# A first unit in another order, two transfers for the constants, and two later loads on another queue

## The chip, the cores and the metric

The kernel runs on one core of one Trainium2 chip. What counts is the device time of one execution in microseconds (us). The same program was timed three times, and the median stands for it. A fourth execution was taken with the hardware profiler, and all rows below come from that one.

## The reference

Three layers follow each other. First comes attention over 4 batches of 8 heads with 576 positions and 64 columns a head; heads 0 to 3 see the last 32 positions, heads 4 to 7 every fourth of the last 128. Then a layer takes the largest of three products, and a second layer uses a quotient of polynomials.

```python
def _attn_ref(q, k, v):
    scores = scale * np.matmul(q, k.transpose(0, 1, 3, 2))
    mask_plain = (rel >= 0) & (rel < window)                                  # window = 32
    mask_dil = (rel >= 0) & (rel < window * dilation) & (rel % dilation == 0) # dilation = 4
    ...
    attn = attn / (np.sum(attn, axis=-1, keepdims=True) + 1e-09)
    return np.matmul(attn, v)

x = _attn_ref(q, k, v)                       # as 2304 rows of 512
h = np.maximum(np.maximum(x @ w1, x @ w2), x @ w3)   # 512 to 768
x = h @ w_out                                        # 768 to 512
h = x @ w_in                                         # 512 to 2048
P = a[0] + a[1] * h + a[2] * h**2 + a[3] * h**3
Q = 1.0 + np.abs(b[0]) * np.abs(h) + np.abs(b[1]) * h**2
out = (P / (Q + 1e-06)) @ w_out2                     # 2048 to 512
```

## The kernel before

The 2304 rows are cut into 12 **chunks** of 192 rows, and two chunks make a **unit** of 384. While the matrix products of a unit run, the attention of the next one is mixed in between them. The first unit has nothing before it, so its order is written out by hand: `START` is a string of steps, and the program walks through it and issues each step's instructions on the engines that the step needs. Every engine then works its own instructions strictly in that order, and waits only for data. Chunks 0 and 1 are the first unit; chunks 2 and 3, which the second unit needs, are also done in `START`. From the second unit on, the order comes from the table `UNIT` and the loop behind it.

The names of the steps, where `c` is a chunk, `p` the plain heads, `d` the dilated ones:

- `Sc:g` scores on TensorE (lines 283 and 295). `MXc`, `Dc`, `SMc` are the maximum, the subtraction and the sum on VectorE (lines 321, 337, 356), `Ec` the exponential on ScalarE (345, 349), `SBc` the division by the sum on VectorE (363) or, with `act`, on ScalarE (367). `Xc` transposes on TensorE (374), `XCc` copies the result back (385, or 383 on VectorE). `Vc` multiplies by the values (397, 405); `VHc` and `VLc` split the outcome into a high and a low part on ScalarE (417) and VectorE (421).
- `L`, `up`, `bits`, `hi`, `lo` bring in one of the 24 weight blocks of the first two products. They come as 64-bit words of 512 KB: `L` loads on SyncE's queue (475), `up` (ScalarE, 488), `bits` (VectorE, two instructions, 494 and 496), `hi` (ScalarE, 510) and `lo` (VectorE, 518) turn them into a high and a low 32-bit part.
- `P:i` is one of the 18 groups of 12 products of 384 columns in the first unit (lines 535 to 537); `H:i` does half of one, the 192 columns of chunk 0 alone, and then `P:i` does only the other half. `M`, `HH`, `HL` take the largest (554, 556) and split it (560, 565). `Y` is the product by the fourth weight, 18 products each, `YS` its copy (589).
- `W:n` puts 4n products of a zero tile, `warm`, in front of the next step's own (line 180). Their result is overwritten.
- `qp`, `qd`, `kp`, `kd`, `k`, `v`, `mk` are loads of queries, keys, values and constants. `kp0` and `kp1` are the two parts of batch 0's plain keys.

SyncE's queue has eight semaphores for its transfers, taken in turn: the transfer n+8 is issued when transfer n has landed. Queries of chunks 4 and 5 and keys of batch 2 go out on GpSimd's queue, from calls that stand behind `START`.

Of the kernel before, what the change touches and what calls it, by code (L numbers as in the profile page):

```python
# [7 lines left out]
F32 = mybir.dt.float32  # L8
# [4 lines left out]
BF16 = mybir.dt.bfloat16  # L13
# [20 lines left out]


START = """
qp0 kp0 mk L W:19 S0:p,mm qd0 kd0 up MX0:p bits L E0:p qd1 hi W:10 S0:d,mm SM0:p L up lo
SB0:p,act MX0:d W:1 S1:d,sc qp1 D0:d bits kp1 E0:d X0:p,0,mm up X0:p,1,mm SM0:d v0 XC0:p,0 MX1:d
XC0:p,1 SB0:d W:9 S1:p,mm E1:d bits v1 W:1 X0:d,0,tp MX1:p W:2 V0:p,pv XC0:d,0 SB1:d hi W:2 X0:d,1,sc L
VH0:p D1:p W:1 X1:d,1,pv XC0:d,1 X1:d,0,tp XC1:d,1 VL0:p W:1 V0:d,mm L E1:p lo XC1:d,0 SM1:p L up  # L40
W:1 V1:d,pv SB1:p VH0:d up L VL0:d W:2 X1:p,0,mm VH1:d X1:p,1,sc bits XC1:p,0 H:0 L XC1:p,1 VL1:d hi
bits V1:p,mm L hi H:1 lo VH1:p qp2 VL1:p up lo hi P:0 k1 bits up S2:p,sc M:0 bits hi lo hi H:2
qd2 MX2:p up bits qd3 E2:p P:1 L lo M:1 P:2 lo L up hi S2:d,sc bits up L SB2:p,act bits P:3 L lo
hi M:2 L lo HH:0 P:4 hi HL:0 L M:3 lo up MX2:d up v3 M:4 P:5 up bits E2:d bits L P:6 bits hi L
hi M:5 X2:p,1,sc M:6 lo P:7 L XC2:p,1 lo up HH:1 L bits up X2:p,0,sc hi HL:1 P:8 v2 M:7 hi bits
XC2:p,0 SB2:d,act lo S3:d,sc lo L M:8 P:9 hi MX3:d L HH:2 lo up HL:2 L up bits X2:d,1,tp M:9
P:10 hi bits L XC2:d,1 lo hi qp3 X2:d,0,tp up M:10 P:11 L bits up XC2:d,0 E3:d bits P:12 M:11
SM3:d HH:3 hi HL:3 hi V2:p,sc lo M:12 P:13 up lo VH2:p bits up VL2:p hi V2:d,sc M:13 SB3:d,act
bits P:14 lo hi lo VH2:d lo up X3:d,0,mm M:14 P:15 XC3:d,0 bits HH:4 up HL:4 hi bits X3:d,1,pv
M:15 P:16 up lo hi bits hi M:16 P:17 lo VL2:d lo S3:p,sc M:17 XC3:d,1,dve HH:5 HL:5 V3:d,mm  # L50
MX3:p E3:p Y:0 VH3:d SM3:p SB3:p VL3:d X3:p,1,tp YS:0 Y:1 XC3:p,1 X3:p,0,sc YS:1 Y:2 XC3:p,0,dve
V3:p,mm YS:2 Y:3 VH3:p VL3:p YS:3
"""

UNIT = """
# [26 lines left out]
def kernel(  # L82
# [15 lines left out]
    nc = tc.nc  # L98
    B, H, S, D = BATCH, HEADS, SEQ, DIM
# [29 lines left out]
    QA = 2  # L129
# [14 lines left out]
    const = ctx.enter_context(tc.tile_pool(name="const", bufs=1))  # L144
# [51 lines left out]
    def load_k(b, part=None):  # L196

        if b not in at_k:
            at_k[b] = (
                at.tile([128, S // 32, 2, 32], F32, tag="kTp", bufs=2, name=f"kTp{b}"),  # L200
                at.tile([128, 8, S // 4], F32, tag="kTd", bufs=2, name=f"kTd{b}"),
            )
        kTp, kTd = at_k[b]
        queue = nc.sync if b < 2 else nc.gpsimd
        for k, cut in ((0, slice(0, CH // 32)), (2, slice(CH // 32, S // 32))):
            if part in (None, k):
                queue.dma_start(out=kTp[:, cut].rearrange("p n a t -> p (n a t)"),
                                in_=kp_in[b][:, 64 * cut.start:64 * cut.stop])
        if part in (None, 1):
            queue.dma_start(out=kTd.rearrange("p n m -> p (n m)"), in_=kd_in[b])  # L210

    def load_q(c, g):
        if c >= NCH:
            return
        queue = nc.sync if c < 2 * QA else nc.gpsimd
        if g == "p":
            t = at.tile([128, 2 * BP, 2 * QP], F32, tag="qTp", bufs=QA, name=f"qTp{c}")
            queue.dma_start(out=t.rearrange("p n w -> p (n w)"), in_=qp_in[c])
        else:
            t = at.tile([128, 8, 2 * M], F32, tag="qTd", bufs=QA, name=f"qTd{c}")  # L220
            queue.dma_start(out=t.rearrange("p n w -> p (n w)"), in_=qd_in[c])
        at_raw[c, g] = t
# [399 lines left out]
    with ExitStack():  # L622
        nc.scalar.preload_act_table_set("natural_log_exp_and_others")
        warm = const.tile([128, 128], BF16, name="warm")
        nc.vector.memset(warm, 0.0)
        mk = const.tile([128, 512], F32, name="mk")
        ident = mk[:, 0:128]
        mk16 = mk[:, 128:384].bitcast(BF16)
        mkd16 = mk[:2 * M, 384:512].bitcast(BF16)
        ident16 = mk16[:, 0:128]  # L630
        mP16 = mk16[:, 128:128 + BP * WP].rearrange("p (i w) -> p i w", i=BP)
        mD16 = mkd16[:, 0:2 * WD].rearrange("p (i w) -> p i w", i=2)
        co = mk[:, 464:470]
# [242 lines left out]
def _laid_out(inputs):  # L876

    import numpy as np

    q, k, v = inputs["q"], inputs["k"], inputs["v"]  # L880
    B, H, S, D = q.shape
    NP, CH, QP, M = H // 2, CHUNK, 64, CHUNK // 4
    BP, NC, WP, WD = CH // QP, S // CH, QP + 32, M + 32
    out = {}
    mk = np.zeros((128, 128 + BP * WP + 2 * WD), np.float32)
    mk[:, 0:128] = np.eye(128, dtype=np.float32)
    for i in range(BP):
# [5 lines left out]
    mk16 = np.zeros((128, 1024), np.int16)
    mk16[:, 0:256] = mk[:, 0:128].copy().view(np.int16)
    mk16[:, 256:256 + 128 + BP * WP] = _bf16(np, mk[:, 0:128 + BP * WP])
    mk16[0:2 * M, 768:768 + 2 * WD] = _bf16(np, mk[0:2 * M, 128 + BP * WP:])
# [77 lines left out]
```

## Time and profile before

| | us |
|---|---|
| median of three runs | 797.05 (796.89 to 797.38) |
| profiled execution, its own time | 796.7 |
| span of the profiled execution | 794.9 |
| TensorE busy | 788.3 |
| VectorE busy | 597.8 |
| ScalarE busy | 466.8 |

The span is what the profile covers from its first to its last record; the execution's own time holds 1.8 us more. TensorE is busy in 99% of the span, but its fillers count as busy, too, and its products overlap, so this share doesn't tell how much of the time is needed work.

### The profile page before, as it was taken

How to read it: one execution, taken by the hardware profiler on the slowest of the kernel's cores; microseconds unless marked ns; L12 is line 12 of the kernel's file. 1: busy time of each engine (PE TensorE's matmuls, PEld its weight loads, DVE VectorE, ACT ScalarE, POOL GpSimd, SP SyncE). 2: the span in 40 equal slices, each digit the busy share in tenths (PEclk: the TensorE clock that was granted, in tenths of full speed). 3: DMA queues.
4: the chain of work that ended last, by engine and by line, in shares of the span. 5: the costliest groups of instructions: out<-in, count | busy, mean ns of one | idle time of the engine just before them, and what ended most of it. 6: DMA issues, size and time to landing. Idle time of an engine off the chain costs nothing.

```text
span 794.9 us, 12837 instructions
## 1 busy us (share of the span) xinstructions
PE 788.3 (99%) x4976; PEld 721.6 (91%) x4976; DVE 597.8 (75%) x1068; ACT 466.8 (59%) x907; POOL 59.1 (7%) x113
## 2 busy tenths in 40 slices
PE   9999999999999999999999999999999999999998
PEld 9999999999999999999978888888888889999996
DVE  5999275566476565548299998888988888998996
ACT  5897232333333333255398768666786677777775
POOL 0100111211211111000100001000010001000000
PEclk9999999999999999999999999999999999999999
DMA  9992346655465454164500011000110011001001
GB/s 342 404 407 80 106 147 215 215 180 190 162 200 186 160 186 164 37 241 158 178 14 1 1 53 54 1 1 0 40 54 0 1 40 53 1 1 40 1 0 40
DMA packets 28061, 86.55 MB, mean 109 GB/s; under 512 B 3648, under 2 KB 4928, under 8 KB 28000
## 3 DMA queue, kind: packets, MB, share of 16 engines
q1 hardware_dynamic: 19056, 52.70, 18.8%
q0 software_dynamic: 8944, 33.04, 11.7%
q8 instruction: 39, 0.64, 0.3%
q14 instruction: 22, 0.18, 0.1%
HBM read 67.90 MB, written 17.83 MB: 108 GB/s over the span
## 4 chain that ended last, share of the span: by engine, by line
PE 80%; issue 10%; DVE 4%; ACT 3%; DMA 1%; POOL 1%; POOLq 0%; ACTq 0%; DVEq 0%; SPq 0%
PE acc L819 8%; PE acc L820 8%; PE acc L821 8%; PE mm L535 8%; PE mm L537 8%; PE mm L536 8%; PE h L537 8%; PE h L535 8%; PE h L536 8%; PE sc L295 3%; PE tpp L374 2%; PE sc L180 1%; PE pv L397 1%; PE pv L405 1%; DVE cvt L496 1%
## 5 line engine op out<-in xcount | busy, mean ns | idle before, releaser
L535 PE MATMUL mm<-x1h,w1s 128*128 128x384 f32 (+1 forms) x444 | 150.1, 339 | 0.0
L537 PE MATMUL mm<-x1h,w1s 128*128 128x384 f32 (+1 forms) x444 | 147.2, 332 | 0.0
L536 PE MATMUL mm<-x1l,w1s 128*128 128x384 f32 (+1 forms) x444 | 147.1, 331 | 0.0
L535 PE MATMUL h<-x2h,w2s 128*128 128x512 f32 (+1 forms) x320 | 118.0, 369 | 0.0
L537 PE MATMUL h<-x2h,w2s 128*128 128x512 f32 (+1 forms) x320 | 118.0, 369 | 0.0
L536 PE MATMUL h<-x2l,w2s 128*128 128x512 f32 (+1 forms) x320 | 117.7, 368 | 0.0
L819 PE MATMUL acc<-w2s,gh 128*128 128x512 f32 x288 | 112.8, 392 | 0.5 <-ACT gh L800 0.5
L820 PE MATMUL acc<-w2s,gh 128*128 128x512 f32 x288 | 113.1, 393 | 0.0
L821 PE MATMUL acc<-w2s,gl 128*128 128x512 f32 x288 | 109.0, 389 | 0.0
L768 ACT ACTIVATE q<-h 128x512 f32<-128x512 f32 (+1 forms) x80 | 44.4, 555 | 89.7 <-PE h L537 86.6
L535 PEld LDWEIGHTS mm<-x1h,w1s 128*128 128x128 f32 x444 | 83.2, 188 | 0.6
L536 PEld LDWEIGHTS mm<-x1l,w1s 128*128 128x128 f32 x444 | 83.6, 188 | 0.0
L537 PEld LDWEIGHTS mm<-x1h,w1s 128*128 128x128 f32 x444 | 83.4, 188 | 0.0
L775 DVE SCALAR_TENSOR_TENSOR q<-q,cs,ab 128x512 f32<-128x512 f32 (+1 forms) x80 | 55.8, 697 | 36.3 <-ACT ab L769 35.8
L535 PEld LDWEIGHTS h<-x2h,w2s 128*128 128x128 f32 x320 | 60.1, 188 | 9.1
L536 PEld LDWEIGHTS h<-x2l,w2s 128*128 128x128 f32 x320 | 60.1, 188 | 8.8
L537 PEld LDWEIGHTS h<-x2h,w2s 128*128 128x128 f32 x320 | 60.0, 188 | 7.8
L821 PEld LDWEIGHTS acc<-w2s,gl 128*128 128x128 f32 x288 | 54.1, 188 | 11.9
L819 PEld LDWEIGHTS acc<-w2s,gh 128*128 128x128 f32 x288 | 54.0, 188 | 11.6 <-ACT gh L800 0.9
L556 DVE TENSOR_TENSOR m<-mm,m 128x384 f32<-128x384 f32 x72 | 39.9, 554 | 31.5 <-PE mm L537 30.4
L820 PEld LDWEIGHTS acc<-w2s,gh 128*128 128x128 f32 x288 | 54.1, 188 | 9.9
L770 ACT ACTIVATE p<-h,cs 128x512 f32<-128x512 f32 (+1 forms) x80 | 59.1, 739 | 0.0
(100 smaller groups left out, 1441.3 us busy)
## 6 DMA issues: line engine op xcount, KB each, us to landing
w1r<-in_w_dram SPq DMA_DIRECT2D x18, 512.0 KB, 9.6
raw<-in_w_in_dram SPq DMA_DIRECT2D x16, 512.0 KB, 3.4
w2d<-cvt POOLq DMA_DIRECT2D x32, 256.0 KB, 2.5
raw<-in_w_out_dram SPq DMA_DIRECT2D x16, 512.0 KB, 3.5
w2s<-w2d SPq DMA_DIRECT2D x32, 256.0 KB, 4.7
x2d<-xs POOLq DMA_DIRECT2D x24, 192.0 KB, 2.4
vd<-in_vd_dram POOLq DMA_DIRECT2D x8, 512.0 KB, 5.0
out_dram<-ob POOLq DMA_DIRECT2D x15, 256.0 KB, 2.7
```

Of the source, the lines that this page charges most:

```text
L295: nc.tensor.matmul(o, lhsT=lq, rhs=rk, start=not pem, stop=not pem or n % G == G - 1)
L374: nc.tensor.transpose(tp[:, i, :], sv[:, G * j + i, :], ident[:Q, :Q])
L535: nc.tensor.matmul(o, lhsT=lh, rhs=rh, start=(i == 0), stop=False)
L536: nc.tensor.matmul(o, lhsT=lh, rhs=rl, start=False, stop=False)
L537: pe_at[0] = nc.tensor.matmul(o, lhsT=ll, rhs=rh, start=False, stop=(i == n - 1))
L556: nc.vector.tensor_tensor(out=m1[u, f], in0=o, in1=m1[u, f], op=ALU.max)
L768: nc.scalar.activation(out=s["q"], in_=s["h"], func=AF.Square)
L770: nc.scalar.activation(out=s["p"], in_=s["h"], func=AF.Identity, scale=cs[:, 3:4], bias=cs[:, 2:3])
L775: nc.vector.scalar_tensor_tensor(out=s["q"], in0=s["q"], scalar=cs[:, 5:6], in1=s["ab"], op0=ALU.mult, op1=ALU.add)
L819: nc.tensor.matmul(o, lhsT=gh, rhs=w[:, 0:512], start=(c == 0), stop=False)
L820: nc.tensor.matmul(o, lhsT=gh, rhs=w[:, 512:1024], start=False, stop=False)
L821: nc.tensor.matmul(o, lhsT=gl, rhs=w[:, 0:512], start=False, stop=(c == F2 - 1))
```

## The change

The kernel after has four edits.

1. `START` holds the same steps in another order. It has 31 instead of 49 `W` units (124 instead of 196 fillers), and no `H`: each of the 18 product groups runs with 384 columns at once. `SB2:d` moves from ScalarE to VectorE, `SB3:p` from VectorE to ScalarE, and two copies of chunk 3's transposes from VectorE to ScalarE.
2. The constants come in two transfers: masks and the 16-bit identity first (`mk`, 208 words a row), the 32-bit identity, the dilated mask and the coefficients second (`mkB`, 214 words a row), where there was one of 512 words.
3. Queries of chunks 4 and 5 and keys of batch 2 are issued on SyncE's queue instead of GpSimd's.
4. The tile `cs` has 24 instead of 8 words a row, so that the tiles of the left-hand pools stand 64 bytes further on.

```diff
 START = """
-qp0 kp0 mk L W:19 S0:p,mm qd0 kd0 up MX0:p bits L E0:p qd1 hi W:10 S0:d,mm SM0:p L up lo
...
+mk qp0 mkB kp0 W:14 S0:p qd0 MX0:p kd0 kp1 E0:p W:7 S0:d,mm qp1 SM0:p SB0:p,act MX0:d D0:d W:1 S1:p
...
@@ load_k
-        queue = nc.sync if b < 2 else nc.gpsimd
+        queue = nc.sync if b < 3 else nc.gpsimd
@@ load_q
-        queue = nc.sync if c < 2 * QA else nc.gpsimd
+        queue = nc.sync if c < 3 * QA else nc.gpsimd
@@
+        CUT = (128 + BP * WP) // 2
+        CW = CUT + 128 + WD + 6
         mk = const.tile([128, 512], F32, name="mk")
-        ident = mk[:, 0:128]
-        mk16 = mk[:, 128:384].bitcast(BF16)
-        mkd16 = mk[:2 * M, 384:512].bitcast(BF16)
+        mk16 = mk[:, 0:CUT].bitcast(BF16)
...
+        ident = mk[:, CUT:CUT + 128]
...
-            "mk": lambda: nc.sync.dma_start(out=mk, in_=consts),
+            "mk": lambda: nc.sync.dma_start(out=mk[:, 0:CUT], in_=consts[:, 0:CUT]),
+            "mkB": lambda: nc.sync.dma_start(out=mk[:, CUT:CW], in_=consts[:, CUT:CW]),
...
-        cs = const.tile([128, 8], F32, name="cs")
+        cs = const.tile([128, 24], F32, name="cs")
```

The lines of the kernel after are one lower than those of before (475 becomes 474, and so on).

SyncE's queue at the start of the program, before; `w1r` is a weight block, `kTp` and `kTd`, `qTp` and `qTd` keys and queries, plain and dilated, `vp` and `vd` the values, and the second number of a shape counts words a row.

```order
L218 DMA qTp_141<-in_qp_dram 128x768
L207 DMA kTp_143<-in_kp_dram 128x384
L635 DMA mk<-in_consts_dram 128x512
L475 DMA w1r_0_147<-in_w_dram 128x512
L221 DMA qTd_241<-in_qd_dram 128x768
L210 DMA kTd_144<-in_kd_dram 128x1152
L475 DMA w1r_1_251<-in_w_dram 128x512
L221 DMA qTd_259<-in_qd_dram 128x768
L475 DMA w1r_2_319<-in_w_dram 128x512
L218 DMA qTp_352<-in_qp_dram 128x768
L207 DMA kTp_143<-in_kp_dram 128x768
L237 DMA vp_371<-in_vp_dram 128x768
```

The same queue at the same place in the kernel after.

```order
L635 DMA mk<-in_consts_dram 128x208
L217 DMA qTp_142<-in_qp_dram 128x768
L636 DMA mk<-in_consts_dram 128x214
L206 DMA kTp_145<-in_kp_dram 128x384
L220 DMA qTd_220<-in_qd_dram 128x768
L209 DMA kTd_146<-in_kd_dram 128x1152
L206 DMA kTp_145<-in_kp_dram 128x768
L217 DMA qTp_276<-in_qp_dram 128x768
L220 DMA qTd_307<-in_qd_dram 128x768
L474 DMA w1r_0_334<-in_w_dram 128x512
L474 DMA w1r_1_340<-in_w_dram 128x512
L474 DMA w1r_2_342<-in_w_dram 128x512
```

All keys and queries of chunks 0 and 1 now stand ahead of the first weight block, which was fourth and is tenth.

VectorE from its first maximum on, before; `mx`, `sm`, `sb` are the maximum, the sum and the scores, `cvt` is a weight block being converted.

```order
L321 TENSOR_REDUCE mx<-sc 128x3 x2
L324 TENSOR_SCALAR mx<-mx 128x6
L494 TENSOR_SCALAR cvt<-cvt 128x512
L496 SCALAR_TENSOR_TENSOR cvt<-w1r_0_147,cvt 128x512
L356 TENSOR_REDUCE sm<-sb 128x6
L518 TENSOR_TENSOR w1s_0_261<-cvt,w1s_0_261 128x512
L360 TENSOR_SCALAR sm<-sm 128x6
L361 RECIPROCAL sm<-sm 128x6
L321 TENSOR_REDUCE mx<-sc 96x4 x2
L337 TENSOR_TENSOR sb<-sc,mx 96x4x48 x2
```

VectorE from its first maximum on, after; `spare` holds the scores of chunk 1.

```order
L320 TENSOR_REDUCE mx<-sc 128x3 x2
L323 TENSOR_SCALAR mx<-mx 128x6
L355 TENSOR_REDUCE sm<-sb 128x6
L359 TENSOR_SCALAR sm<-sm 128x6
L360 RECIPROCAL sm<-sm 128x6
L320 TENSOR_REDUCE mx<-sc 96x4 x2
L336 TENSOR_TENSOR sb<-sc,mx 96x4x48 x2
L320 TENSOR_REDUCE mx<-sc 128x3 x2
L336 TENSOR_TENSOR spare<-sc,mx 128x288 x2
L355 TENSOR_REDUCE sm<-sb 96x8
```

The conversion of the first block stood behind the first maximum; now the softmax of both chunks goes ahead of it.

TensorE at the end of `START`, before; `hh` and `hl` are the two parts of the largest, `wo1s` the fourth weight, and the last row is the second unit's first product.

```order
L295 MATMUL sc<-kTp_680,qTp_1079 128x96 x6
L405 MATMUL pv<-pt,vd_864 64x3x16 x16
L535 MATMUL mm<-hh_831,wo1s_1141 128x384
...
L374 MATMUL tpp<-mk,sb 96x128 x3
...
L397 MATMUL pv<-pt,vp_862 64x64 x12
...
L535 MATMUL mm<-x1h_689,w1s_0_261 128x384
```

TensorE at the end of `START`, after.

```order
L536 MATMUL mm<-x1h_149,w1s_2_1068 128x384
L404 MATMUL pv<-pt,vd_1084 64x3x16 x16
L396 MATMUL pv<-pt,vp_1082 64x64 x12
L534 MATMUL mm<-hh_730,wo1s_1104 128x384
...
L534 MATMUL mm<-x1h_529,w1s_0_489 128x384
```

Scores, transposes and values of chunk 3's plain heads stood among the four `Y`; now all attention ends ahead of the first `Y`, and nothing but `Y` stands between it and the second unit. From there on TensorE's rows are the same in both kernels.

## Rows read from the trace of the kernel before

**Rows 1.** Who TensorE waited for, whole span: total us, times, longest us.

```profile
PE sc L180 <- DVE warm L625: 1.0, 1, 1.0
PE tpp L374 <- DVE sb L363: 0.8, 1, 0.8
PE acc L819 <- ACT gh L800: 0.5, 1, 0.5
PE tpp L374 <- ACT pt L385: 0.4, 1, 0.4
```

**Rows 2.** Stretches: length, busy us (instructions) of each engine, granted clock, DMA share, GB/s.

```profile
1.00:5.00 4.00, 4.00 (x38) 4.00 (x39) 0.00 (x0) 1.02 (x1) 0.00 (x0) 1.00 0.77 228
5.00:7.00 2.00, 2.00 (x39) 2.00 (x37) 0.40 (x3) 0.00 (x0) 0.00 (x0) 1.00 0.96 336
25.58:78.77 53.19, 52.77 (x442) 50.76 (x441) 50.19 (x104) 44.14 (x122) 3.47 (x7) 1.00 0.73 289
```

**Rows 3.** TensorE's timeline: start us, us, line, operation.

```profile
0.99 6.31 PE L180 MATMUL sc<-warm 128*128 128x128 bf16 x76 [0.99 <-DVE warm L625]
7.14 0.41 PE L283 MATMUL sc<-mk 128*128 128x288 bf16 x2
...
26.08 0.33 PE L535 MATMUL mm<-x1h,w1s 128*128 128x192 f32 x1
...
27.57 0.92 PE L397 MATMUL pv<-pt,vp 96*64 96x64 f32 x24
...
31.19 0.42 PE L283 MATMUL sc<-mk 128*128 128x288 bf16 x2
...
32.70 0.34 PE L535 MATMUL mm<-x1h,w1s 128*128 128x192 f32 x1
...
36.78 0.43 PE L283 MATMUL sc<-mk 96*96 96x320 bf16 x2
...
38.36 0.42 PE L535 MATMUL mm<-x1h,w1s 128*128 128x384 f32 x1
...
46.79 0.49 PE L374 MATMUL tpp<-mk,sb 128*96 128x128 f32 x3
...
94.67 0.33 PE L535 MATMUL mm<-x1h,w1s 128*128 128x384 f32 x1
```

**Rows 4.** Transfers issued near 1.2 to 3.1 us: KB each, us from issue to landing.

```profile
kTp<-in_kp_dram SPq DMA_DIRECT2D x1, 192.0 KB, 3.1
mk<-in_consts_dram SPq DMA_DIRECT2D x1, 256.0 KB, 4.4
kTd<-in_kd_dram SPq DMA_DIRECT2D x1, 576.0 KB, 7.6
```

**Rows 5.** SyncE's queue in order of time: start us, us of the issue.

```profile
1.66 0.42 SPq L635 DMA_DIRECT2D mk<-in_consts_dram x1
2.12 0.43 SPq L475 DMA_DIRECT2D w1r<-in_w_dram x1
...
3.07 0.43 SPq L210 DMA_DIRECT2D kTd<-in_kd_dram x1
...
19.55 0.33 SPq L218 DMA_DIRECT2D qTp<-in_qp_dram x1
```

**Rows 6.** VectorE's timeline at the prices of its steps.

```profile
24.44 0.76 DVE L363 TENSOR_TENSOR spare<-spare,sm 128x576 f32<-128x576 f32 x1
...
35.64 0.56 DVE L556 TENSOR_TENSOR m<-mm,m 128x384 f32<-128x384 f32 x1
36.11 0.68 DVE L518 TENSOR_TENSOR w1s<-cvt,w1s 128x512 fp32r<-128x512 f32 x1
36.71 0.42 DVE L494 TENSOR_SCALAR cvt<-cvt 128x512 int32<-128x512 int32 x1
...
37.77 0.17 DVE L360 TENSOR_SCALAR sm<-sm 128x6 f32<-128x6 f32 x1
...
42.20 0.88 DVE L321 TENSOR_REDUCE mx<-sc 96x4 f32<-96x320 f32 x2
```

More of the change, by code (lines that the diff above doesn't have):

```diff
@@ L36 @@
 START = """
-qp0 kp0 mk L W:19 S0:p,mm qd0 kd0 up MX0:p bits L E0:p qd1 hi W:10 S0:d,mm SM0:p L up lo
[L38 to L52, printed above, removed]
+mk qp0 mkB kp0 W:14 S0:p qd0 MX0:p kd0 kp1 E0:p W:7 S0:d,mm qp1 SM0:p SB0:p,act MX0:d D0:d W:1 S1:p
@@ new lines @@
+qd1 S1:d,pv E0:d X0:p,1,mm MX1:p X0:p,0,mm L up D1:p L L SM0:d E1:p MX1:d v0 SM1:p SB0:d SB1:p v1
+XC0:p,1 qp2 L W:8 X0:d,1,mm up X0:d,0 XC0:p,0 W:1 X1:p,1,sc V0:p,mm X1:p,0,sc qd2 bits L L E1:d
+XC0:d,0 XC0:d,1 V0:d,mm up XC1:p,0 XC1:p,1 L SB1:d hi bits k1 X1:d,1,pv bits VH0:p VH0:d L qp3
+V1:p,tp X1:d,0,pv S2:p L hi lo XC1:d,1 VL0:p XC1:d,0 qd3 lo VL0:d up V1:d,mm VH1:p bits hi VH1:d
+VL1:p hi VL1:d lo S2:d,pv L P:0 L up MX2:d bits up P:1 E2:d lo bits M:0 up MX2:p M:1 P:2 SB2:d hi
+P:3 L X2:d,0,mm E2:p hi X2:d,1 bits L L M:2 lo hi lo up lo bits up HH:0 L hi bits L S3:d up lo
@@ new lines @@
+XC2:d,1 S3:p,pv bits up M:3 hi XC2:d,0 bits L hi lo P:6 M:6 P:4 hi P:5 up SB2:p,act MX3:d lo bits L
+v2 lo up hi MX3:p P:7 M:4 E3:d bits P:9 M:5 up lo X2:p,0 up XC2:p,0 SM3:d bits M:7 M:9 hi hi
+SB3:d,act lo HL:0 P:10 bits P:8 L lo X2:p,1,sc M:10 hi M:8 up up lo P:12 E3:p up bits L L bits hi
+P:13 SM3:p L bits lo M:12 hi P:14 HH:1 XC2:p,1 L P:15 lo up hi up HL:1 SB3:p,act v3 M:13 bits P:16
+M:15 hi M:14 V2:d,sc X3:d,0,mm lo up X3:d,1,pv HH:2 bits lo up hi M:16 XC3:d,0 P:11 bits hi XC3:d,1
+X3:p,0 HH:4 bits V2:p,sc X3:p,1,mm P:17 lo L lo M:11 up bits up HL:2 XC3:p,0 hi XC3:p,1 bits M:17
@@ L53 @@
+HH:3 hi HH:5 lo VH2:p lo HL:4 hi HL:3 lo V3:d V3:p,tp HL:5 VH2:d VH3:d VH3:p VL2:d Y:0 YS:0 Y:1 Y:2
+Y:3 VL3:p VL2:p YS:1 YS:2 VL3:d YS:3
 """
@@ L625 @@
         nc.vector.memset(warm, 0.0)
+        CUT = (128 + BP * WP) // 2
+        CW = CUT + 128 + WD + 6
         mk = const.tile([128, 512], F32, name="mk")
-        ident = mk[:, 0:128]
-        mk16 = mk[:, 128:384].bitcast(BF16)
-        mkd16 = mk[:2 * M, 384:512].bitcast(BF16)
+        mk16 = mk[:, 0:CUT].bitcast(BF16)
         ident16 = mk16[:, 0:128]
         mP16 = mk16[:, 128:128 + BP * WP].rearrange("p (i w) -> p i w", i=BP)
-        mD16 = mkd16[:, 0:2 * WD].rearrange("p (i w) -> p i w", i=2)
-        co = mk[:, 464:470]
+        ident = mk[:, CUT:CUT + 128]
+        mD16 = mk[:2 * M, CUT + 128:CUT + 128 + WD].bitcast(BF16).rearrange("p (i w) -> p i w", i=2)
+        co = mk[:, CUT + 128 + WD:CW]
         loads = {
-            "mk": lambda: nc.sync.dma_start(out=mk, in_=consts),
+            "mk": lambda: nc.sync.dma_start(out=mk[:, 0:CUT], in_=consts[:, 0:CUT]),
+            "mkB": lambda: nc.sync.dma_start(out=mk[:, CUT:CW], in_=consts[:, CUT:CW]),
             "kp0": lambda: load_k(0, 0), "kd0": lambda: load_k(0, 1), "kp1": lambda: load_k(0, 2),
@@ L892, in _laid_out @@
         mk[:2 * M, 128 + BP * WP + WD * i:128 + BP * WP + WD * i + WD] = np.concatenate([band, band])
[L893 to L896, printed above, removed]
+    cut = 128 + BP * WP
+    mk16 = np.zeros((128, cut + 256 + 2 * WD + 12), np.int16)
+    mk16[:, 0:cut] = _bf16(np, mk[:, 0:cut])
+    mk16[:, cut:cut + 256] = mk[:, 0:128].copy().view(np.int16)
+    mk16[0:2 * M, cut + 256:cut + 256 + 2 * WD] = _bf16(np, mk[0:2 * M, cut:])
     consts = mk16.view(np.float32)
-    consts[:, 464:468] = inputs["moe2_a"]
-    consts[:, 468:470] = inputs["moe2_b"]
+    at = (cut + 256 + 2 * WD) // 2
+    consts[:, at:at + 4] = inputs["moe2_a"]
+    consts[:, at + 4:at + 6] = inputs["moe2_b"]
     out["consts"] = consts
```

## The prediction

> **What bounds the kernel now.** I read the list of TensorE's waits first, then the stretches, then TensorE's own timeline, and VectorE's last.
>
> In the whole span TensorE waits four times for 2.7 us [rows 1], and none of it lies in the middle of the span. So after the first unit nothing but TensorE's own work sets the time, and whatever the first unit saves or loses is kept to the end, as long as its rows stay the same there. They do.
>
> In the first unit the picture has three parts [rows 3]. From 0.99 to 7.14 TensorE runs 76 fillers and waits for the first keys and queries. From 7.14 to 26.08 it does the attention of chunks 0 and 1 with fillers between the steps: the softmax on VectorE and ScalarE and the loads set the pace, and TensorE has little to do. From 26.08, where the first half group `H:0` starts, to 94.67, where the second unit's first product starts, it works without a gap but for two waits of 0.8 and 0.4 us [rows 1]. In almost the same stretch, 25.58 to 78.77, VectorE is busy 50.2 of 53.2 us [rows 2]. Two engines are thus nearly full here, and a change is worth what it brings on the later of the two.
>
> **The change part by part.**
>
> *Start.* 38 fillers stand between 1 and 5 us, 39 between 5 and 7 [rows 2]: 9.5 and 19.5 in a us. The granted clock reads 1.00 in both, so this is the step from 1.2 to 2.4 GHz after a stretch of steady products. 56 fillers in place of 76 end at 5.0 + 18/19.5 = 5.9. The scores `S0:p` also need the first keys, now the fourth transfer, issued where the weight block stood at 2.12 [rows 5]. At best it lands after the keys' own 3.1 us [rows 4], at 5.2; at worst like the old constants, with about the same bytes ahead, at 1.66 + 4.4 = 6.1 [rows 4, 5]. I take 6.0, 1.1 us earlier than 7.14.
>
> *Loads of the attention.* Before, 2.36 MB were issued up to the dilated keys, which landed at 3.07 + 7.6 = 10.7 [rows 4, 5]. The transfer issued at 19.55 is the 22nd, which waited for the 14th, so 5.90 MB had landed at 19.5 [rows 5]. That is 2.49 us for one MB. After, the bytes up to the dilated keys are 1.79 MB, so they land at 9.2; up to the plain queries of chunk 1, 2.58 MB, 11.2; up to its dilated ones, 2.97 MB, 12.2; the first weight block at 13.5, the values between 17 and 21.
>
> *The chain to the first full group.* A plain scores step takes 32.70 - 31.19 = 1.5 us, a dilated one 38.36 - 36.78 = 1.6 [rows 3]. `S1:p` starts at 11.2 with its queries and ends at 12.8, `S1:d` ends at 14.4. VectorE has then done the softmax steps that it could, and from 14.6 on it has no gap to `VL1:d`, the last thing that `P:0` needs. Its steps there, by their prices [rows 6]: `MX1:d` 0.88 and a small one, 1.0; `SM1:p`, priced as a maximum over its 576 columns, 0.8; `SB0:d`, `SB1:p`, `SB1:d`, scaled by columns from 0.76 with two small ones of 0.17, 0.85 + 1.1 + 1.2; four `bits` of 37.77 - 36.71 = 1.06, 4.2; two `lo` of 0.60, 1.2; four `VL`, priced as the `M` of the same 384 columns, 35.64 to 36.11, 0.47 each, 1.9. Together 12.25, so `P:0` starts at 26.9. TensorE is there in time: its steps of both chunks and `S2` make 15.7 us (six scores 9.3, eight transposes of about 0.3, four value steps of about 1), the 17 `W` behind the first 3.8, and 6.0 + 19.5 = 25.5.
>
> *What is left from there.* Before, 94.67 - 26.08 = 68.6 [rows 3]. Off go the two waits, 1.2; `V1:p`, 0.9, and the two scores of chunk 2, 3.1, which now stand ahead of `P:0`; and the halves: 36 products of 192 columns take 36.78 - 32.70 = 4.08, 0.113 each, 48 of 384 columns take 46.79 - 38.36 = 8.43, 0.176 each [rows 3], so 72 of the one cost 8.16 where 36 of the other cost 6.32, 1.8 more. 61.6 us remain. Without a wait the second unit starts at 26.9 + 61.6 = 88.5, 6.2 earlier.
>
> *VectorE's deadline.* The four `Y` now stand last, 18 products of 0.176 each, 12.6 together. The sixth sixth of the first one needs `HL:5` and the last `lo`: at 88.5 - 12.6 + 2.6 = 78.5. From 26.9 VectorE has 20 `bits` (21.2), 22 `lo` (13.2), 12 `M` and 6 `HL` (8.5) and the softmax of chunks 2 and 3 (7.0, four maxima 3.3, `SB2:d` 1.2, two sums 1.3, three pairs of small ones 1.2): 49.9, done at 76.8 if it never waits. Before, it stood idle 3.0 us of a like stretch [rows 2], mostly in small waits for ScalarE, which is busy 44.1 of the 53.2. Bounds: no idle time, no wait; 3.0 us, done at 79.8 and TensorE waits 1.3. I take 2.2, nearer to the row, since the order is new but the pairs of `up`, `bits`, `hi`, `lo` are the same: 0.5 us of waiting. The middle is as tight: `P:15` can start near 61.7, and its `lo` is done near 61.1 plus the idle time up to there.
>
> *Costed at nothing.* The moved copies, `SB2:d` and `SB3:p`: they are in the sums above on VectorE; ScalarE gives up one scaling in eight parts and gets one in six and two copies, about as much, and its 53.2 - 44.1 = 9 us of idle time [rows 2] cover the rest. The queries and keys on SyncE's queue: 2.75 MB behind the last weight block. All loads of `START` are 22.1 MB, so that block lands near 10.7 + 19.8 x 2.49 = 60, the moved ones near 67; the second unit asks for them after 88, so 20 us cover it, and the next weights behind them are asked for later still. If that cover were gone, the second unit's first scores would wait up to 7 us. The weight blocks come later at first (13.5), but the `lo` of the last has some 15 us in hand. The split constants: one issue more, 0.4 us on the queue [rows 5], in the 6.0 above; VectorE's coefficients need the second part, which lands ahead of the keys. The 64 bytes: no row shows the same operation on a tile at another offset, shapes and counts stay; I take nothing, with a few tenths either way.
>
> **Sum.** Start of the second unit: 88.5 + 0.5 = 89.0 for 94.67, 5.7 less. Against the profiled execution: span 794.9 - 5.7 = 789.2, its own time 791.0. It lies 0.35 below the median, so the median comes out at 791.3.
>
> **Rivals.**
>
> *VectorE falls further behind.* Its 6.2 us of gain hang on a new order in which each engine waits for the other's step. Each us of idle time beyond 1.7 is a us for TensorE. With 4 to 6 us it is 793.2 to 795.2; with 8 the gain is gone. For it: 94% busy, three engines in a row for each block. Against it: 3.0 us before, with the same steps.
>
> *The clock falls (the other side).* With 72 fillers gone, TensorE stands still more often between 6 and 27 us. If it fell back to the slow pace there, 9.5 for 19.5 fillers [rows 2], the 19.5 us of steps and fillers would take 39 and `P:0` would start at 45: 18 us later, 89 + 18 = 107, 809. It decides against the change once `P:0` starts after 26.9 + 5.7 = 32.6, that is, when some 7 us of work run at the slow pace (its slack of 1.4 us off). Against it: by the steps above the gaps are about 1.4 us in 21, and before, the pace held across the two waits. The Trainium skill, TensorE: Matmul & The Clock Gate, Part 1, says that the array's clock is gated down by default and again after idling, and wants products kept flowing; by that rule thinner fillers could bring these 18 us, by the rows they bring nothing. The trace here agrees as to the first rise and shows no fall.
>
> *Earlier than I think.* If the transfers land up to 1.5 us sooner (3.1 us after issue, as the first), VectorE and TensorE both shift: 789.8.
>
> *It does nothing.* VectorE does the same work as before and was done with `HL:5` at 78.8, where the stretch of [rows 2] ends, by my sum at 79.0. If it set the end of the unit, nothing would change: 797. It doesn't, since behind `HL:5` TensorE had 15.9 us before, with chunk 3's plain heads among the `Y`, and has 10.
>
> **How the numbers follow.** The forecast, idle time of 1 to 3.5 us, 0.56: 790.6 to 792.7. Earlier, 0.10. VectorE behind by 3.5 to 6, 0.18; by more, up to no gain, 0.08. No change 0.02. Clock 0.04, and 0.02 for some other loss. A measurement can tell 0.2%, 1.6 us, from no change, so 795.5 to 798.6 counts as the same. Faster 0.87, same 0.08, slower 0.05. The range of 8 in 10 leaves out the clock, the nothing and the farther half of VectorE's lag: 789.8 to 794.3.
>
> **What would show it.** Right: `S0:p` near 6, the first full group near 27, the second unit's first product near 89, and in TensorE's waits one of about half a us before a `Y` product. Wrong: waits of TensorE for `lo` from the middle of the unit on, above 2 us together; fillers or scores at the slow pace after 6 us; a first full group after 28.5; a later stretch whose products take longer than before.

## The result and the profile after

The changed kernel takes 788.55 us (median of four executions, 788.26 to 789.44); the kernel before took 796.97 beside it (796.81 to 797.38). The ratio is 0.9894, with a 95% interval from 0.9882 to 0.9906. The gain is 8.4 us where 5.7 was forecast, and the time lies 1.25 us below the range of 789.8 to 794.3: the sign and the mechanism were right, the size was not.

The list of TensorE's waits over the whole span of the changed kernel (us in total, times, longest); it answers to [rows 1]:

```profile
PE sc L179 <- DVE warm L624: 1.0, 1, 1.0
PE sc L294 <- DMA kTp<-in_kp_dram: 0.3, 1, 0.3
PE acc L820 <- ACT gh L801: 0.2, 1, 0.2
PE tpp L373 <- DVE sb L362: 0.2, 1, 0.2
```

The two waits inside the first unit are gone, and the wait before a `Y` that I expected is not there. TensorE's timeline of the changed kernel (start us, us, line, operation), which answers to [rows 3]:

```profile
0.99 4.99 PE L179 MATMUL sc<-warm 128*128 128x128 bf16 x56 [0.99 <-DVE warm L624]
5.82 0.41 PE L282 MATMUL sc<-mk 128*128 128x288 bf16 x2
6.52 1.55 PE L294 MATMUL sc<-kTp,qTp 128*128 128x96 f32 x12 [0.29 <-DMA kTp<-in_kp_dram]
...
11.18 0.41 PE L282 MATMUL sc<-mk 128*128 128x288 bf16 x2
...
27.13 0.42 PE L534 MATMUL mm<-x1h,w1s 128*128 128x384 f32 x1
27.39 0.34 PE L535 MATMUL mm<-x1l,w1s 128*128 128x384 f32 x1
27.56 0.35 PE L536 MATMUL mm<-x1h,w1s 128*128 128x384 f32 x1
...
87.27 0.33 PE L534 MATMUL mm<-x1h,w1s 128*128 128x384 f32 x1
```

The first scores step starts at 5.82 (its products with the keys at 6.52), `S1:p` at 11.18, the first full group at 27.13 and the second unit's first product at 87.27, for 6.0, 11.2, 26.9 and 89.0 in the forecast. Note the pace behind a step of the attention: the product at 27.13 is followed after 0.26 us, the next after 0.17. That small thing comes back below.

The 8.4 us against the 5.7, term by term, from the two profiled executions: `P:0` 0.2 later than forecast; from there to the second unit 60.1 us in place of 61.6, 1.4 better; no wait before `Y`, 0.5 better; and behind the second unit's first product 786.5 - 87.27 = 699.2 us (786.5 is the span), where the kernel before took 794.9 - 94.67 = 700.2: 1.0 better in a part that I had costed at nothing. Together 2.7.

VectorE in two stretches of the changed kernel (columns as in [rows 2]), and the last of its first-unit steps:

```profile
14.50:26.63 12.13, 11.87 (x203) 10.63 (x201) 11.75 (x28) 11.42 (x37) 0.00 (x0) 1.00 1.03 404
27.13:76.55 49.42, 49.42 (x402) 48.28 (x401) 48.25 (x103) 44.23 (x126) 0.00 (x0) 1.00 0.78 308
```

```profile
76.08 0.55 DVE L564 TENSOR_TENSOR hl<-m,hh 128x384 fp32r<-128x384 f32 x1
76.55 1.94 DVE L420 TENSOR_TENSOR x1l<-pv,x1h 128x384 fp32r<-128x384 f32 x4
```

From `MX1:d` to the last `VL` it takes 12.1 us, 12.25 forecast. From 27.13 it is busy 48.25 of 49.42 us and done with `HL:5` at 76.6, the end of the row at 76.08. The first product that reads it is the 17th of the first `Y`:

```profile
77.56 0.33 PE L535 MATMUL mm<-hl,wo1s 128*128 128x384 f32 x1
```

So it has 0.9 us in hand at the end, where I had it 0.5 late.

In the second layer, the same 220 us of the kernel before and of the changed one, each without a gap (columns as in [rows 2]; the first x is TensorE's products). First before:

```profile
420.00:640.00 220.00, 220.00 (x965) 180.94 (x965) 196.36 (x301) 159.75 (x262) 4.28 (x8) 1.00 0.05 19
```

Then after:

```profile
420.00:640.00 220.00, 220.00 (x972) 182.19 (x971) 196.12 (x300) 159.95 (x263) 4.27 (x8) 1.00 0.06 19
```

972 products where there were 965: 226.3 ns each for 228.0, at the same granted clock, with no wait in either.

### The profile page after: what moved, and what is told of

The parts are those of the page before. It is cut to its first block, busy times and chain, and to the rows that moved or that the text cites. A ratio compares the mean times of both kernels' runs of the same rounds, so it can differ in the third digit from the quotient of the medians.

```text
span 786.5 us, 12629 instructions
## 1 busy us (share of the span) xinstructions
PE 780.8 (99%) x4868; PEld 715.8 (91%) x4868; DVE 594.8 (76%) x1066; ACT 464.7 (59%) x907; POOL 55.6 (7%) x106
## 4 chain that ended last, share of the span: by engine, by line
PE 84%; issue 10%; DVE 2%; DMA 2%; POOL 1%; ACT 1%; SPq 0%; POOLq 0%; ACTq 0%; DVEq 0%
PE mm L534 10%; PE mm L536 9%; PE mm L535 9%; PE acc L821 8%; PE acc L822 8%; PE acc L820 8%; PE h L534 8%; PE h L536 8%; PE h L535 8%; PE sc L294 3%; PE tpp L373 2%; PE pv L404 1%; PE pv L396 1%; DMA kTp<-in_kp_dram 1%; DMA raw<-in_w_out_dram 1%
## 5 line engine op out<-in xcount | busy, mean ns | idle before, releaser
L534 PE MATMUL mm<-x1h,w1s 128*128 128x384 f32 x432 | 146.9, 341 | 0.0
L536 PE MATMUL mm<-x1h,w1s 128*128 128x384 f32 x432 | 144.5, 334 | 0.0
L535 PE MATMUL mm<-x1l,w1s 128*128 128x384 f32 x432 | 144.5, 334 | 0.0
L534 PEld LDWEIGHTS mm<-x1h,w1s 128*128 128x128 f32 x432 | 80.9, 188 | 0.4
L535 PEld LDWEIGHTS mm<-x1l,w1s 128*128 128x128 f32 x432 | 81.2, 188 | 0.0
L536 PEld LDWEIGHTS mm<-x1h,w1s 128*128 128x128 f32 x432 | 81.1, 188 | 0.0
L534 PEld LDWEIGHTS h<-x2h,w2s 128*128 128x128 f32 x320 | 60.1, 188 | 8.8
L535 PEld LDWEIGHTS h<-x2l,w2s 128*128 128x128 f32 x320 | 60.1, 188 | 8.8
L536 PEld LDWEIGHTS h<-x2h,w2s 128*128 128x128 f32 x320 | 60.1, 188 | 7.5
```

The costliest lines, as they stand in the source:

```text
L534: nc.tensor.matmul(o, lhsT=lh, rhs=rh, start=(i == 0), stop=False)
L535: nc.tensor.matmul(o, lhsT=lh, rhs=rl, start=False, stop=False)
L536: pe_at[0] = nc.tensor.matmul(o, lhsT=ll, rhs=rh, start=False, stop=(i == n - 1))
```

## The experiments

Each kernel ran beside the kernel before, whose median was 797.0 to 797.1 in all of them.

**The 64 bytes.** In this first kernel the change's last edit is undone:

```diff
-        cs = const.tile([128, 24], F32, name="cs")
+        cs = const.tile([128, 8], F32, name="cs")
```

> The changed kernel with the tile of small constants back at 32 bytes a partition, so that every tile behind it in the left half of the memory lies 64 bytes lower, as before the change. Nothing else differs. If the 1.0 us that the later stages gained comes from these 64 bytes, the later stages take 700.2 us again in place of 699.2, the products of the second layer are 229 ns apart in place of 227, and the time is 789.5. If it comes from other timing (when loads, VectorE and ScalarE work beside the products), the pace stays at 227 and the time within 0.2 of 788.5. The first unit's last product should end at 87.1 in either case if only the later stages feel the offset; if the first unit's 60.1 us feel it too, some 0.3 us later.

789.30 us (788.84 to 789.78; ratio 0.9899, 0.9886 to 0.9912). The medians alone, 0.75 apart, hardly tell it from the changed kernel; the trace does. There are 965 products between 420 and 640 again, and the later stages take 699.9 us, 0.7 more. Its first full group stood at 27.47, and from there to the second unit it took 60.1 as before: the first unit doesn't feel the bytes.

The second is the kernel before with this edit alone (8 to 24):

> The kernel before with that tile alone enlarged to 96 bytes a partition. If the 64 bytes carry the 1.0 us of the later stages, this kernel takes 796.0 us against 797.0, with the second unit's first product still at 94.7 (or up to 0.3 earlier, if the first unit feels the offset). If they do nothing, it takes 797.0.

796.29 us against 797.07 (ratio 0.9991, 0.9982 to 0.9999). The second unit starts at 94.48 and the later stages take 793.7 - 94.48 = 699.2. Its row of that stretch has the changed kernel's count:

```profile
420.00:640.00 220.00, 220.00 (x972) 182.25 (x971) 197.84 (x302) 160.18 (x263) 4.27 (x8) 1.00 0.05 19
```

The third goes 64 bytes further (24 to 40):

> The changed kernel with that tile at 160 bytes a partition, so that the tiles behind it lie 64 bytes higher still, 128 above where they were before the change. If what counts is where a tile stands within 128 bytes, this is the same as 32 bytes: 789.5 and 229 ns between products. If any shift does it by way of chance timing, or if 64 bytes do nothing, no such relation: 788.5, or a value of its own.

792.94 us (792.53 to 793.20), 955 products in the stretch, 4.4 us more than the changed kernel: no period of 128 bytes. The place matters more than this change showed, and it can cost as easily as it gains.

Two kernels then move only the second layer's working tiles, by a pad ahead of their pool:

```diff
+        pad = ctx.enter_context(tc.tile_pool(name="pad", bufs=1))
+        pad.tile([128, 16], F32, name="pad")
         wk = ctx.enter_context(tc.tile_pool(name="wk", bufs=2, reuse_waits="tile"))
```

> The changed kernel with 64 unused bytes a partition ahead of the second layer's working tiles alone (q, ab, p, r, gh, gl, ob): they stand where they stood with 160 bytes of constants, everything else where the change put it. With 160 bytes the products into acc were 232 ns apart in place of 227 in the 512-column tiles, and the kernel took 4.4 us longer than the changed one. If the place of gh and gl (and of what VectorE and ScalarE read and write beside the products) makes the pace, the acc products are 232 ns apart again and the time is 792 to 792.5. If the place of the left-half weight blocks, of x1h, x1l and of the first layer's weights makes it, the time stays at 788.5 and the pace at 227.

794.33 us (793.69 to 794.96), 954 products. The working tiles carry all of it, and 1.4 us more than when every tile behind `cs` moved with them (792.94); which of the other tiles gives that back was not followed. With 32 words of pad in place of 16:

> The changed kernel with 128 unused bytes a partition ahead of the second layer's working tiles, where 64 cost 5.8 us. The offsets tried so far, in bytes above those of the changed kernel, gave 229 ns between acc products at -64, 227 at 0, 232 at +64 in the 512-column tiles. If the pace repeats every 128 bytes it is 227 again and the time 788.5, but -64 and +64 differ already, so this is unlikely; if every 256 bytes, +128 is a place of its own: anything from 788 to 794. If it only grows with the distance above 0, more than 794.3.

794.28 us, 952 products: as slow, neither back to the start nor further up.

Which of the working tiles? `gh` and `gl` get a pool `gk` of their own, and the pad stands ahead of it, behind `wk`; in the second kernel `gk` comes first, and the pad stands between it and `wk`:

```diff
         wk = ctx.enter_context(tc.tile_pool(name="wk", bufs=2, reuse_waits="tile"))
+        pad = ctx.enter_context(tc.tile_pool(name="pad", bufs=1))
+        pad.tile([128, 16], F32, name="pad")
+        gk = ctx.enter_context(tc.tile_pool(name="gk", bufs=2, reuse_waits="tile"))
...
-            s["gh"] = wt(s, "gh", 4, F32R)
+            s["gh"] = wt(s, "gh", 4, F32R, gk)
...
-            s["gl"] = wt(s, "gl", 4, F32R)
+            s["gl"] = wt(s, "gl", 4, F32R, gk)
```

> The changed kernel with gh and gl (the weights of the acc products) in a pool of their own, 64 bytes a partition higher within 256; q, ab, p, r and ob stay where they stood within 256. Moved together, all of these cost 5.8 us. If the place of what the acc products themselves load decides, this kernel takes 794 with about 954 products in the 220 us from 420 to 640. If the place of the tiles decides that VectorE and ScalarE read and write beside the products, it takes 788.5 with 972.

> The counterpart: q, ab, p, r and ob 64 bytes a partition higher within 256, gh and gl where they stood within 256. If the products' own weights decide, 788.5 and 972 products between 420 and 640; if the tiles of VectorE and ScalarE decide, 794 and 954. If it is the place of the one against the other, both this kernel and the one before it are slow.

793.73 us (793.36 to 794.68) for the first, 788.86 (788.42 to 789.47) for the second. The stretch with `gh` and `gl` moved:

```profile
420.00:640.00 220.00, 220.00 (x953) 178.77 (x952) 192.72 (x295) 157.67 (x259) 4.26 (x8) 1.00 0.05 19
```

And with everything but them moved:

```profile
420.00:640.00 220.00, 220.00 (x972) 182.25 (x971) 195.96 (x300) 159.43 (x264) 4.26 (x8) 1.00 0.06 19
```

So it is the place of `gh` and `gl`, which TensorE loads as weights, and not that of the other tiles that VectorE and ScalarE use beside them. But the loading itself isn't shown to be the cause: ScalarE also writes `gh`, and VectorE reads it and writes `gl`. And some of the products into `h` are slower, too, though they load neither. Of each kind one line between 420 and 640 us (count, then ns: shortest, median, longest), first from the changed kernel:

```profile
L820 PE MATMUL acc<-w2s,gh x164: 389/389/389, 420.7 to 639.6; 128*128 128x512 f32 x164
L536 PE MATMUL h<-x2h,w2s x159: 389/389/389, 423.9 to 637.4; 128*128 128x512 f32 x159
```

Then from the one with `gh` and `gl` moved:

```profile
L823 PE MATMUL acc<-w2s,gh x160: 393/398/398, 420.7 to 638.5; 128*128 128x512 f32 x160
L536 PE MATMUL h<-x2h,w2s x156: 388/393/397, 424.0 to 639.6; 128*128 128x512 f32 x156
```

The Trainium skill, SBUF — State Buffer, section "SBUF: two separate sides", says that TensorE, ScalarE and VectorE's own ports never wait on one another there; the kernel with the neighbours moved agrees, at 972 products. Why the offset of `gh` and `gl` changes the pace no run shows.

**The queue.** The queries and keys of the later parts go back to GpSimd's queue:

```diff
-        queue = nc.sync if b < 3 else nc.gpsimd
+        queue = nc.sync if b < 2 else nc.gpsimd
...
-        queue = nc.sync if c < 3 * QA else nc.gpsimd
+        queue = nc.sync if c < 2 * QA else nc.gpsimd
```

> The changed kernel with the queries and keys of chunks 4 and 5 and of the third part back on GpSimd's queue. I costed this edit at nothing: 788.5 within 0.3, the second unit's first product at 87.3. The rival: on GpSimd's queue these 2.75 MB land among the weight blocks, each of the blocks behind them comes up to 2.5 us a MB later, VectorE's conversions with them, and a wait of TensorE appears before a group of the first unit: up to 2 us more, 790.5, with such a wait in the list.

796.39 us (793.83 to 797.49; ratio 0.9985, 0.9976 to 0.9995): nearly the whole gain is lost. Neither number fits. The rival had the crowding right, but put the wait before a product group, behind late weight blocks, and not at the queries of chunk 3, and it had a quarter of the price. The profiled execution, at 793.83 the lowest of the twelve, shows two longer waits of TensorE:

```profile
PE sc L294 <- DMA qTd<-in_qd_dram: 3.4, 1, 3.4
...
PE sc L294 <- DMA kTp<-in_kp_dram: 0.8, 1, 0.8
```

The first is chunk 3's dilated scores; around it the timeline of TensorE, and below it its stretches (columns as in [rows 2]):

```profile
40.34 1.53 PE L294 MATMUL sc<-kTd,qTd 128*96 128x48 f32 x16 [3.38 <-DMA qTd<-in_qd_dram]
41.70 0.41 PE L282 MATMUL sc<-mk 128*128 128x288 bf16 x2
41.95 2.66 PE L294 MATMUL sc<-kTp,qTp 128*128 128x96 f32 x12
```

```profile
40.00:42.00 2.00, 1.67 (x19) 1.67 (x20) 1.48 (x3) 1.15 (x3) 0.00 (x0) 1.00 1.03 410
42.00:44.00 2.00, 2.00 (x12) 2.00 (x11) 1.55 (x3) 1.72 (x5) 0.61 (x1) 0.50 1.03 410
44.00:46.00 2.00, 2.00 (x10) 2.00 (x10) 1.94 (x6) 1.31 (x3) 0.54 (x1) 0.65 1.03 410
```

On GpSimd's queue, which has nothing ahead of them, five of these seven loads, 1.97 MB, are issued between 25.2 and 29.7 us, around the dilated queries of chunk 3 at 26.3, with the DMA engines full. These queries land 13.9 us after their issue, in the changed kernel 8.7. And the wait doesn't end with itself: TensorE stood still for 3.4 us, the granted clock then reads 0.50 from 42 to 44, and a plain scores step that takes 1.55 at 6.52 of the changed kernel takes 2.66. From the first full group to the second unit it is 65.3 us: 60.1, 3.5 for the wait, from start to start, and 1.7 for the clock. Ten of the twelve executions took longer, 795.59 to 797.49, at a mean granted clock of 0.992 to 0.996 where the profiled one has 0.998; a longer stretch at the low clock would fit, but no trace of them shows it.

The same edit the other way round, alone in the kernel before:

> The kernel before with only the move of chunk 4's and 5's queries and of the third part's keys to SyncE's queue. In the changed kernel's order this move saves a wait of 3.4 us for chunk 3's dilated queries, and with it a stretch at the slow clock. In the order before, chunk 3's dilated scores start at 51.6 and not at 36.6, and TensorE waits for no load: theory, 797.0 within 0.3, the move is worth something only together with the new order. If these transfers took bandwidth from the weight blocks in the order before too, its waits of 0.8 and 0.4 us go or shrink, and the time is 795.8 to 796.7.

796.97 us against 797.11 (ratio 0.9998, 0.9990 to 1.0007), with the waits of 0.8 and 0.4 us still there. The move is worth nothing in the old order, where chunk 3's dilated scores start at 51.6, and nearly everything in the new one, where they stand at 36.2.

**The fillers behind the first scores.** `W:7`, `W:1`, `W:8` and `W:1` are taken out:

```diff
-mk qp0 mkB kp0 W:14 S0:p qd0 MX0:p kd0 kp1 E0:p W:7 S0:d,mm qp1 SM0:p SB0:p,act MX0:d D0:d W:1 S1:p
+mk qp0 mkB kp0 W:14 S0:p qd0 MX0:p kd0 kp1 E0:p S0:d,mm qp1 SM0:p SB0:p,act MX0:d D0:d S1:p
...
-XC0:p,1 qp2 L W:8 X0:d,1,mm up X0:d,0 XC0:p,0 W:1 X1:p,1,sc V0:p,mm X1:p,0,sc qd2 bits L L E1:d
+XC0:p,1 qp2 L X0:d,1,mm up X0:d,0 XC0:p,0 X1:p,1,sc V0:p,mm X1:p,0,sc qd2 bits L L E1:d
```

> The changed kernel without the 68 fillers behind the first scores (W:7, W:1, W:8, W:1); the 56 at the start stay. Theory: VectorE sets the first full group, the fillers are only time that TensorE has to spare, and the clock holds through gaps of some us, so 788.5, at most 0.3 less. The rival of the clock: TensorE now stands still for about 3.5 us more between 6 and 27, in gaps of up to 2 us; if that brings it back to the slow level, the granted clock reads near 0.5 there, the steps take twice as long, and the first full group comes up to 18 us later: 790 to 806.

A median of 795.75 us over twelve executions from 788.64 to 798.40. Two of the twelve, 788.64 and 789.15, had a mean granted clock of 1.000; the others 0.985 to 0.995. The profiled one took 797.31; its stretches:

```profile
15.00:17.00 2.00, 0.00 (x0) 0.00 (x0) 1.93 (x7) 2.00 (x6) 0.00 (x0) 1.00 1.04 401
17.00:20.00 3.00, 2.20 (x15) 1.87 (x17) 2.83 (x9) 2.98 (x18) 0.00 (x0) 0.52 1.03 405
20.00:27.00 7.00, 7.00 (x92) 6.03 (x91) 5.33 (x10) 3.84 (x9) 0.00 (x0) 0.50 1.03 404
27.00:35.00 8.00, 8.00 (x66) 7.59 (x64) 3.23 (x6) 4.16 (x8) 0.00 (x0) 0.50 1.03 406
```

From before 15 to after 17 us TensorE stands still, in a wait of 2.9 us for `SB0:d`. By itself this would cost next to nothing: the two executions at 1.000 lie within 0.6 us of the changed kernel's median. But then the clock reads 0.50, 1.2 GHz, up to 35 us and beyond, and the first full group starts at 34.94 in place of 27.13. Both theories had a case each: where the clock holds, the fillers cost nothing; where it doesn't, the rival's loss is there. The Trainium skill, TensorE: Matmul & The Clock Gate, Part 1, says that idling gates the array's clock down and that sustained work is needed to raise it; these rows and those of the queue agree, and the changed kernel, whose granted clock reads 1.00 from 5 to 40 us, has the fillers in these places.

**Changeovers.** The groups 3, 4, 11, 17 and the first `Y` are cut in pieces that stand between attention steps (`G:n,a,b` and `Z:c,a,b` are products a to b of a group):

```diff
-P:3 L X2:d,0,mm E2:p hi X2:d,1
+G:3,0,9 L X2:d,0,mm G:3,9,12 E2:p hi X2:d,1
...
-V2:d,sc X3:d,0,mm lo up X3:d,1,pv
+V2:d,sc G:11,0,4 X3:d,0,mm lo G:11,4,8 up X3:d,1,pv G:11,8,10
```

> The changed kernel with seven more changeovers: the groups 3, 4, 11, 17 and the first Y are cut into pieces that stand between the attention steps, which come one after the other in the changed kernel. The same products and steps, nothing added. Between the first full product and the second unit the kernel before had 16 stretches of attention steps among the products and 2.5 us that neither the steps, nor waits, nor products at 0.111 and 0.173 account for; the changed one has 6 and 1.0 us: 0.16 a changeover. If that is what I left out of what remains behind the first full group, seven more cost 1.1 us: second unit's first product at 88.4, time 789.6. If changeovers cost nothing and the gain of 1.4 came from elsewhere, 87.3 and 788.5.

789.98 us (789.40 to 790.13). From the first full group to the second unit 61.6 us, 1.5 more. Part of this is a wait that the cutting brought, of a product for VectorE's `m`:

```profile
47.86 0.34 PE L536 MATMUL mm<-x1h,w1s 128*128 128x384 f32 x1
48.88 0.44 PE L534 MATMUL mm<-x1h,w1s 128*128 128x384 f32 x1 [0.68 <-DVE m L576]
49.17 0.34 PE L535 MATMUL mm<-x1l,w1s 128*128 128x384 f32 x1
```

The list has 0.68 us for it, since it counts from the end of the product before. From start to start it is 1.02 where the steady pace is 0.173, and the next product follows after 0.29: 1.0 us lost. That leaves 0.5 us for seven changeovers, less than 0.08 each. Changeovers cost something, but half of the price.

The two traces of before and after account for the 1.4 us themselves. Beyond the steady paces of 0.173 and 0.111, the starts of the products in this stretch lose 1.7 us before, with 16 changeovers, and 0.7 after, with 6; the steps give another 0.1. That is 1.1 us. The remaining 0.3 lie in the two waits that went, which the prediction took from the list as 1.2. In the kernel before, the first pair shows such a step without a wait:

```profile
55.10 0.34 PE L537 MATMUL mm<-x1h,w1s 128*128 128x384 f32 x1
55.27 0.49 PE L374 MATMUL tpp<-mk,sb 96*80 96x96 f32 x4
...
57.57 0.34 PE L537 MATMUL mm<-x1h,w1s 128*128 128x384 f32 x1
58.31 0.53 PE L374 MATMUL tpp<-mk,sb 96*80 96x96 f32 x4 [0.40 <-ACT pt L385]
...
82.42 0.34 PE L537 MATMUL mm<-hh,wo1s 128*128 128x384 f32 x1
83.54 0.51 PE L374 MATMUL tpp<-mk,sb 128*96 128x128 f32 x3 [0.78 <-DVE sb L363]
```

Without a wait the step stands 0.17 behind its product; with one, 0.74 and 1.12: 1.5 us for the two. These 1.1 us are 0.11 a changeover, the cut groups gave less than 0.08; why they differ no run shows.

**Halves.**

```diff
-VL1:p hi VL1:d lo S2:d,pv L P:0 L up MX2:d bits up P:1 E2:d lo bits M:0 up MX2:p M:1 P:2 SB2:d hi
+VL1:p hi VL1:d lo S2:d,pv L H:0 P:0 L up MX2:d bits up H:1 P:1 E2:d lo bits M:0 up MX2:p M:1 H:2 P:2 SB2:d hi
```

> The changed kernel with its first three groups as two halves each, one right behind the other, as before the change in count: 36 products of 384 columns become 72 of 192. By the prices of the prediction this is 1.8 us more of TensorE's work, all of it on the path, since TensorE has no wait behind the first full group: from that group to the second unit 61.9 in place of 60.1, time 790.3. If what I mis-sized in the part that remains is the price of the halves, more than 1.8: up to 2.4, 790.9. If the halves fill waits that the trace doesn't list, less.

790.41 us, and 61.9 us from the first full group to the second unit, for 60.1: 1.8, as priced. This term of the sum was right.

**VectorE's deadline.** `RL:0` repeats the subtraction of `HL:0`:

```diff
-SB3:d,act lo HL:0 P:10
+SB3:d,act lo HL:0 RL:0 RL:0 RL:0 RL:0 P:10
```

> The changed kernel with the subtraction for HL:0 carried out five times in place of once, which adds about 2 us to VectorE's work in the middle of the first unit and changes no value. In the changed kernel's trace VectorE is done with HL:5 at 76.55, and the Y product that reads it is due near 77.3. If VectorE is the second engine that is all but full, with 0.75 us in hand, TensorE now waits about 1.3 us, before a group or before a Y: 789.8. If VectorE has slack that its busy time hides, no wait and 788.5. If the four operations upset the alternation with ScalarE, more than 2 us.

790.92 us (790.30 to 791.52). VectorE has 2.2 us more to do (52.4 us busy up to the second unit for 50.2), and the same way takes TensorE 2.0 us more. The waits, in TensorE's timeline, come in the middle of the unit:

```profile
56.98 0.34 PE L536 MATMUL mm<-x1h,w1s 128*128 128x384 f32 x1
57.97 0.41 PE L534 MATMUL mm<-x1h,w1s 128*128 128x384 f32 x1 [0.66 <-DVE m L555]
...
62.38 0.34 PE L535 MATMUL mm<-x1l,w1s 128*128 128x384 f32 x1
63.40 0.44 PE L536 MATMUL mm<-x1h,w1s 128*128 128x384 f32 x1 [0.68 <-DVE w1s L517]
```

From start to start these two waits cost 0.82 and 0.85 us above the steady 0.173; the products right behind them and a smaller stop at 65.09 cost another 0.3. That is all of the 2.0. So VectorE is the second engine that is all but full: of 2.2 us more it hid 0.2, and the tight place is there, not at `HL:5`.

**The constants in one transfer.**

```diff
-mk qp0 mkB kp0 W:14 S0:p
+mk qp0 kp0 W:14 S0:p
...
-            "mk": lambda: nc.sync.dma_start(out=mk[:, 0:CUT], in_=consts[:, 0:CUT]),
-            "mkB": lambda: nc.sync.dma_start(out=mk[:, CUT:CW], in_=consts[:, CUT:CW]),
+            "mk": lambda: nc.sync.dma_start(out=mk[:, 0:CW], in_=consts),
```

> The changed kernel with its constants in one transfer of 211 KB, issued first, in place of two, and so one issue less ahead of the keys. I costed the split at nothing beyond one issue: the first scores start within 0.3 us of 6.5, and the time within 0.4 of 788.5. If the split is what brings the first landings earlier, the masks that the first scores read land later, the whole chain up to the first full group moves with them, and the time is 789 to 790.

788.45 us (787.73 to 788.92), first full group at 27.26: nothing, as costed.

## Why the prediction was too small

*Start* held to half a us: the step starts at 5.82, but its products with the keys wait until 6.52, 0.4 us behind the bound of 6.1 for the keys. The step in the fillers' pace, 9.5 to 19.5 in a us, is in [rows 2]; the granted clock reads 1.00 on both sides of it, so the clock as its reason isn't in these rows. *Loads of the attention* held, too: the transfers landed some 0.4 us earlier than their forecast times. SyncE's queue shows it, since the transfer n + 8 is issued when n has landed; the first dilated keys, the plain and the dilated queries of chunk 1 and the first weight block were down at:

```profile
8.80 0.33 SPq L238 DMA_DIRECT2D vd<-in_vd_dram  x1
...
10.76 0.33 SPq L238 DMA_DIRECT2D vd<-in_vd_dram  x1
11.81 0.33 SPq L217 DMA_DIRECT2D qTp<-in_qp_dram  x1
13.01 0.33 SPq L474 DMA_DIRECT2D w1r<-in_w_dram  x1
```

*The chain to the first full group* came out at 27.13 for 26.9. VectorE's part was right to 0.2 us; "TensorE is there in time" was wrong: TensorE's steps and fillers take 21.3 us from 5.82 where I had 19.5, it works without a gap from 17.2 to 27.1, and its last step, `S2:d`, and not VectorE, lets `P:0` start. That the number came out near is luck: TensorE and VectorE finish 0.5 us apart.

*What is left from there* is the first step that failed, by 1.4 us. It took off the waits, the moved steps and the halves at the prices of their own rows, and the moved steps and the halves were right. What it left out was what each return from an attention step to the products costs, ten times less often: 1.1 us by the two traces, some 0.75 at the price that the cut groups give. And the two waits were worth 1.5 us and not 1.2. My price of a product, 0.176, was itself an average that held some of these returns; the steady ones stand 0.173 apart.

*VectorE's deadline* failed by the 0.5 us of waiting. The work was 48.25 us and not 49.9, the idle time 1.2 and not 2.2. The picture behind it, two engines nearly full, held: 2 us more for VectorE became 2 us for TensorE.

*Costed at nothing* failed in one term. The 64 bytes were worth 1.0 us in the later stages (0.7 when undone); I had allowed "a few tenths". That it is the place of `gh` and `gl` was shown for 64 bytes further on, not for the step that the change makes. The split constants and the moved loads did cost nothing. But for the loads I had asked only how late they come; what they would run into at their old place under the new order I had not asked, and the answer was 3.4 us of waiting in the list and a fall of the clock behind it.

Of the rivals, VectorE did not fall behind, and the "earlier" case had a share in the landings only. The clock did not fall, but two experiments show that its mechanism is near: where TensorE stood still for 2.9 and 3.4 us, the wait cost more than its own length, and I had priced a us of waiting at a us.

## What to carry to other kernels

Price the returns between small steps and large products as an own term, counted before and after, and take the price of a product from a steady stretch. Where products overlap, read what a wait costs from start to start, with the product behind it: the list, which counts from the end of the one before, had 0.68 us where 1.0 was lost. When an order is changed together with the place of some loads, ask of each edit what the new order would do without it, not only what the edit itself delays. Before calling a shift of addresses nothing, compare the number of products in an equal, gapless stretch of two traces: it showed 0.7% in that stretch, where the medians lay 0.1% apart.

## What the runs showed of the hardware that was not expected

- The pace of the second layer's fp32r products of 512 columns depends on where in a partition `gh` and `gl` lie, which half of them load as weights. With these at -64, 0, +64 and +128 bytes from the changed kernel's place, 965, 972, 953 to 955 and 952 products fit into the same 220 us (228.0, 226.3, 230.4 to 230.9 and 231.1 ns); at -64 and +128 other tiles moved with them. Moving the tiles around them by 64 bytes changed nothing (972). The whole kernel moves between 788.5 and 794.3 us with it.
- A wait of 2.9 or 3.4 us of TensorE was followed by the granted clock at 0.50, in the one kernel for about 3.4 us (0.50 and then 0.65 in two stretches of 2 us), in the other for 18 us and more. Of twelve executions of one kernel, two escaped it.
- The first product behind an attention step is followed after 0.26 us and not 0.17. The whole return costs 0.11 us by the traces of before and after, and less than 0.08 by the cut groups.
- A wait of a product that the list puts at 0.66 to 0.78 us cost 0.8 to 0.95 from start to start.
